# Loading the 64-row remainders of Wq and Wk by 16 heads with their halves swapped, and V rows on GpSimd's queue, in a fused attention and FFN kernel

## The chip, the cores and the metric

The kernel runs on one core of a Trainium2 chip, in one launch. The metric is the device time of that launch in microseconds (us), the median of several runs; lower is better.

The core's engines have names that recur below. PE (TensorE) multiplies matrices, and PEld is its loading of weights. DVE (VectorE), ACT (ScalarE) and POOL (GpSimd) work on elements. SP (SyncE) only issues DMA transfers; ACT and POOL can issue them too. The memory next to the engines has 128 partitions; a transfer or a matmul uses all of them, or a part.

## The reference

Four blocks run in turn on x (2048 rows of 576, bf16): attention, FFN, the same attention and the same FFN again with the same weights. Each takes a layer norm of x and adds its result to x.

```python
def _A_ref(x, mem0, Wq, Wk, Wv, Wo, seg_len):        # 32 heads of 128, seg_len 32, 8 rows of memory
    ...
    mem = mem0
    for s in range(n_seg):                            # 64 segments
        xs = x[:, s * seg_len:(s + 1) * seg_len, :].copy()
        h = jnp.concatenate([mem, xs], axis=1)        # 40 rows
        q = jnp.einsum('btd,dhe->bhte', h, Wq)
        k = jnp.einsum('btd,dhe->bhte', h, Wk)
        v = jnp.einsum('btd,dhe->bhte', h, Wv)
        scores = jnp.einsum('bhqe,bhke->bhqk', q, k) * scale
        scores = jnp.where(mask[None, None], scores, -1000000000.0)
        p = _softmax(scores, axis=-1)
        o = jnp.einsum('bhqk,bhke->bhqe', p, v)
        o = jnp.einsum('bhte,hed->btd', o, Wo)
        mem = o[:, :M, :].copy()
        outs.append(o[:, M:, :])
    return jnp.concatenate(outs, axis=1)

def _B_ref(x, w1, w3, w2):                            # 576 -> 4608 -> 576
    h = _silu(x @ w1) * (x @ w3)                      # shortened
    return h @ w2

x = x + _A_ref(_layernorm(x), A_mem0, ...)
x = x + _B_ref(_layernorm(x), ...)
x = x + _A_ref(_layernorm(x), A_mem0, ...)
x = x + _B_ref(_layernorm(x), ...)
```

The memory rows make the attention a recurrence: a segment needs the output of the one before it.

## The kernel before

**Steps.** One step is one segment of 32 rows. The second attention runs 8 segments behind the first, so that there are 72 steps; in steps 8 to 63 both layers have a segment and their rows stand side by side as the moving side of one matmul (80 columns: twice 8 + 32). The FFN of both layers runs in pieces of 128 rows between the attention's parts.

**One step of attention.** The 32 heads go in four groups of 8 (`g` = 0 to 3). For each group the kernel makes Q and K (`QK` and its remainder `QKt`), the scores, a softmax on DVE and ACT, a transpose of P, PV, and with Wo the output. Where both layers run, P goes into a buffer PB that POOL has filled with zeros (`pb_zero`, a memset of 128x1024 of 0.95 us), DVE multiplies the softmax into it, and SP transposes it by DMA into PTS (`ptr_dma`). PV multiplies PTS with V. There are two buffers each of PB and PTS.

**Rows of 576.** The contraction over 576 rows goes as four full chunks of 128 and a remainder of 64. Wq and Wk lie in the tile W, `[128, 9, 4096]`: chunks 0 to 3 are Wq's full chunks, 4 to 7 Wk's, and chunk 8 holds the remainders: Wq's in partitions 0 to 63, Wk's in 64 to 127, each 4096 columns (32 heads of 128). `qk_tail` (node `QKt`) multiplies them. For each head it issues one matmul on the lower half of PE's rows (Wq) and one on the upper half (Wk); such row-tiled matmuls on different halves can run side by side. The FFN has row-tiled remainders of its own (`FFt`). A group of them in PE's order thus goes lower, upper, lower, upper.

**What sets the order.** `make_nodes` writes the work as nodes with costs and dependencies. PE's order is a fixed string of letters, one for each node. `plan` simulates the engines with the costs and fixes in which order ACT, DVE, POOL and SP issue their nodes; the costs in the nodes move only this order. The program then runs with semaphores.

**Loads.** SP loads the weights at the start in the order of the node's priorities: Wv, the first rows of x (XN), `load_qt` (both remainders of Wq and Wk, two transfers of 64x4096), Wq's and Wk's full chunks for heads 0 to 15 (8 transfers of 128x2048), those for heads 16 to 31, and Wo. The FFN's weights (tiles W13 and W2C; `W<-in_B_w_dram` in the profile, W_83 for W13 in the order's rows) don't stay: SP loads them again and again, on the same queue as the transposes. POOL issues the loads of x for the residual (XR), some stores, and a step of the layer norm (L950).

**V rows.** For the first layer's segments 9 to 16 V is computed ahead and stored in DRAM (XV). `va_load` (node `VAl`, 4 for each of 8 steps, 32 in all, 32x1024 or 64 KB each) loads the rows back into V by SP's queue. A load for step t + 1 and group g waits for PV of step t and group g, which reads the rows that it overwrites.

Of the kernel before, what the change touches and what calls it, by code (L numbers as in the profile page):

```python
# [9 lines left out]
ACT = mybir.ActivationFunctionType  # L10
# [3 lines left out]
P = 128  # L14
R64 = 64
D = 576
NCH = D // R64
H = 32
E = 128
MEM = 8  # L20
SEG = 32
# [5 lines left out]
GROUPS = ((0, 8), (8, 8), (16, 8), (24, 8))  # L27
# [5 lines left out]
R_HT = 6  # L33
PTR = 112
VAT = -9.5
LOAD_BW = {"ldqk": 400e3, "ldv": 410e3, "ldo": 360e3}
AH = (8, 17)
AROWS = (AH[0] + 1) * SEG
TRLAT = 2.5
# [29 lines left out]
def role(t):  # L69

    return (t - LAG) % 2
# [199 lines left out]
def make_nodes(em, nseg, pools, o=Opt, dma_bw=230e3, load_bw=380e3, tail_bw=330e3):  # L271
# [24 lines left out]
    def load(name, nbytes, prio, fn, deps=()):  # L296
        return node("DMA", nbytes / LOAD_BW.get(name, load_bw), fn, deps=deps, prio=prio, name=name, lat=2.0)

    ld_m0 = node("ACT", 0.1, em.load_m0(), prio=-90, name="m0", lat=8.0)
    ld_t = [node("DMA", 1.3, em.load_vt(0), prio=-10.0, name="ldt", lat=2.0), node("ACT", 0.1, em.load_vt(1), prio=-80, name="ldt", lat=9.0)]  # L300
    ld_qt = node("DMA", 3.0, em.load_qt(), prio=-9.2, name="ldt", lat=2.0)
    ld_qk = [load("ldqk", kb(1024, H // 2 * E), i - 9.0, em.load_qk(i)) for i in (0, 1)]
    ld_h = [ld_qk[h0 // (H // 2)] for h0, _ in GROUPS]
    ld_v = [load("ldv", kb(512, 2048), VAT + 0.1 * i, em.load_v(i)) for i in (0, 1)]
# [3 lines left out]
    stored = []  # L308
    b = banks(1)
# [42 lines left out]
    vx_ev, last_v, pvs = {}, [], {}  # L352
# [46 lines left out]
    def step(t):  # L399
# [19 lines left out]
        for g, (h0, nh) in enumerate(GROUPS):  # L419
            qs, qe = [], []  # L420
            for uh, un in units(g, nl):
                q = Slot("qkt", users=1)
                b = banks()
                pq = t + o.qk + o.ustep * uh / 4
                m_ = node("PE", 8 * un * mmq, em.qk(t, uh, un, b), deps=hx + hm[:1] + ([ld_h[g]] if t == 0 else []),
                          prio=pq, mode="full", acq=[q] + b, name="QK")
                n = node("PE", un * mmq, em.qk_tail(t, uh, un, b), deps=hx + hm + ([ld_h[g], ld_qt] if t == 0 else []), prio=pq + o.qkt, mode="row",
                         acq=[q] + b, name="QKt")
# [13 lines left out]
            a = node("DVE", dve(w40), em.sm_add(t, g, s, sme), deps=[sc], prio=pf, rel=[s], name="add")  # L442
            m_ = node("DVE", dve(w40, w40) + 0.13, em.sm_max(t, g, sme), deps=[a], prio=pf, name="maxsub")
            c = node("ACT", 0.105 + w40 * 0.000833, em.sm_exp(t, g, sme), deps=[m_], prio=pf, name="exp")
            pb = Slot("pb")
            d = node("DVE", dve(w40) + 0.23, em.sm_sum(t, g, sme), deps=[c], prio=pf, name="sum")
            w = (1.04 - 0.07 * (e and not pre(t)) if nl == 2 else 0.46) * nh / 8
            pbs = node("DVE", w, em.sm_pb(t, g, sme, pb), deps=[d], prio=pf, acq=[pb], rel=[sme], name="pb")
            pts = Slot("pts")
            if nl == 2:  # L450
                tr = node("DMA", 1.25 * nh / 8, em.ptr_dma(t, g, pb, pts), deps=[pbs], prio=pf - 0.02, acq=[pts], name="TR", lat=TRLAT, ring=TRX)
            else:
                bt = banks(1)
# [12 lines left out]
            ot = [Slot("ot") for _ in range(nl)]  # L466
            if pre(t) and t > AH[0]:
                kept = [d for blk in blks for d in vx_ev["VM", t - 1, blk]]
                if t < AH[1]:
                    kept.append(node("DMA", 0.3, em.va_load(t, g), deps=stored + [pvs[t - 1, g]], prio=t - 1 + o.gstep * g + 0.2, lat=2.4, ring=0.6, name="VAl"))  # L470
            else:
                kept = [d for blk in blks for d in vx_ev["VX", t - e, blk]]
            pv = node("PE", nh * mm80, em.pv(t, g, pts, b), deps=pe_ + kept + [d for blk in blks for d in vx_ev["VM", t, blk]],
                      prio=pf + o.pv, mode="full/col", acq=b + ot, rel=[pts], name="PV")
            pvs[t, g] = pv
            if paired(t):
                for blk in blks:
                    gb, gd = vgs[blk // 2]
                    vx_ev["VX", t + 1, blk] = vg_out(t, blk, gb, gd + [pv], 0)
            ote = [node("AD", ew(w40), em.ot_ev(t, g, ab, b[ab], ot[ab]), deps=[pv], prio=pf, rel=[b[ab]], name="OTe") for ab in range(nl)]  # L480
            wo = node("PE", 4 * nh * mm80, em.wo(t, g, ot), deps=ote + ([ld_o[g]] if t == 0 else []), prio=t + o.wo + o.wog * h0 / 8, mode="full",
                      acq=[y] if g == 0 else [], name="WO")
# [32 lines left out]
    kept = {}  # L515
# [195 lines left out]
class Emitter:  # L711
# [98 lines left out]
        return lambda n: (self.adma if r else self.dma)(self.wv(True)[r * R64:(r + 1) * R64, :].rearrange("p (q n) -> p q n", q=NV),  # L810
                                                        self.a.wv[4 * P:D, :].rearrange("p (q r n) -> r p q n", q=NV, r=2)[r])

    def load_qt(self):
        def f(n):
            for r, wd in ((0, self.a.wq), (1, self.a.wk)):
                self.dma(self.T.W[r * R64:(r + 1) * R64, 8, :], wd[4 * P:D, :])
        return f

    def wv(self, tail):
# [304 lines left out]
    def va_load(self, t, g):  # L1124

        def f(n):
            r0, row = (t - AH[0] - 1) * SEG, 96 * role(t)
            self.dma(self.T.V[row:row + SEG, 2 * g:2 * g + 2, :], self.T.XV[r0:r0 + SEG, g * 1024:(g + 1) * 1024].rearrange("p (b n) -> p b n", n=512))
        return f

    def at(self, t):
# [32 lines left out]
    def qk_tail(self, t, uh, un, b):  # L1164
        def f(n):
            first = self.begin(b)
            for j in range(un):
                e0 = (uh + j) * E
                for kind in (0, 1):
                    rr = slice(kind * R64, (kind + 1) * R64)  # L1170
                    x, w = self.qk_rhs(t, rr, 4)
                    self.mm(self.bk(b[kind])[:, j * w:(j + 1) * w], self.T.W[rr, 8, e0:e0 + E], x,
                            first and j == 0, True, tile_position=(kind * R64, 0))
        return f

    def qk_ev(self, t, un, r, q, b):
# [459 lines left out]
```

## Time and profile before

| | |
|---|---|
| median of 3 runs | 2638.43 us (2637.35 to 2639.35) |
| profiled execution | 2643.07 us |
| its span, first to last instruction | 2641.3 us |
| around the span | 1.8 us |
| mean granted TensorE clock | 0.994 |
| busy: PE / DVE / ACT / POOL | 97% / 77% / 46% / 13% |
| mean DMA rate | 142 GB/s |

The span is cut into views: busy shares of the engines, the chain of work that ended last (followed back from the last instruction to what released each step), groups of instructions, waits, and timelines. L735 is the line through which all matmuls are issued, L741 that of DVE, L738 of ACT, L744 SP's DMAs, L753 POOL's DMAs, L1280 the memset of PB, L1290 the transpose by DMA. In a timeline's row stand the start, the duration, the engine, line and operation, output<-input, the count of like instructions, and in brackets the idle time before and what ended it.

### The profile page before, as it was taken

The numbers are of one execution on the slowest core, as the hardware profiler recorded it, in microseconds if no ns is written. First come the engines' busy times: TensorE is split into PE (matmuls) and PEld (weight loads), VectorE is DVE, ScalarE is ACT, GpSimd is POOL, SyncE is SP. The second block draws the span as 40 slices with busy tenths as digits, with TensorE's granted clock in tenths as the row PEclk, the third lists the DMA queues.
The fourth block names the chain that finished last, engine by engine and source line by source line (L and its number), as shares of the span: only waits on it lengthen the run. The fifth ranks groups of instructions, "written<-read, shape, count | busy, mean of one in ns | idle before, by whom it ended". The sixth has DMA issues, their size and how long they took to land.

```text
span 2641.3 us, 132672 instructions
## 1 busy us (share of the span) xinstructions
PE 2563.1 (97%) x58964; PEld 2182.5 (83%) x58991; DVE 2042.3 (77%) x5156; ACT 1225.3 (46%) x3492; POOL 338.1 (13%) x401
## 2 busy tenths in 40 slices
PE   6999999999999999999999999999999999999998
PEld 4788778888888888888888888888888888888887
DVE  5778777787888778778877877887787777788866
ACT  2545444544445354444535444453544445454543
POOL 1111111110111111111101101111111111011110
PEclk8999999999999999999999999999999999999999
DMA  9155747556555667555464655655575555554457
GB/s 308 56 154 139 183 106 179 143 134 155 129 135 115 151 127 155 134 132 138 110 144 126 158 137 126 146 112 139 120 166 134 135 135 112 135 121 141 127 156 239
DMA packets 690960, 375.94 MB, mean 142 GB/s; under 512 B 234728, under 2 KB 683248, under 8 KB 690128
## 3 DMA queue, kind: packets, MB, share of 16 engines
q1 hardware_dynamic: 686784, 359.94, 55.6%
q8 instruction: 461, 7.55, 1.2%
q0 software_dynamic: 3024, 6.93, 1.0%
q14 instruction: 115, 0.94, 0.1%
q10 hardware_dynamic: 576, 0.57, 0.1%
HBM read 309.11 MB, written 4.46 MB: 119 GB/s over the span
## 4 chain that ended last, share of the span: by engine, by line
PE 86%; DMA 7%; DVE 5%; issue 1%; ACT 1%; SPq 0%; POOL 0%; ACTq 0%; DVEq 0%; POOLq 0%
PE bank L735 86%; DMA PTS<-PB 2%; DMA W<-in_B_w_dram 1%; DMA W<-in_A_Wk_dram 1%; DVE STAT L741 1%; DMA W2C<-in_B_w_dram 1%; DVE SME L741 1%; DVE PB L741 1%; DVE V L741 1%; DVE HTT L741 1%; DMA WV<-in_A_Wv_dram 0%; ACT V L738 0%; SPq L744 0%; DVE QKT L741 0%; DVE XR L741 0%
## 5 line engine op out<-in xcount | busy, mean ns | idle before, releaser
L735 PEld LDWEIGHTS <-W 128*128 128x128 bf16 (+2 forms) x31776 | 1241.3, 100 | 131.8 <-issue 68.6
L735 PE MATMUL bank<-HT,W 128*128 128x80 bf16 (+2 forms) x23040 | 792.0, 197 | 16.6 <-issue 6.1
L735 PE MATMUL bank<-XTB,W 128*64 128x256 bf16 (+5 forms) x8736 | 661.4, 263 | 5.9 <-DMA W<-in_B_w_dram 3.1
L1280 POOL MEMSET PB<- 128x1024 bf16 x288 | 273.7, 951 | 1728.1 <-DMA PTS<-PB 950.9
L738 ACT ACTIVATE QKT<-bank 128x192 bf16<-128x192 f32 (+2 forms) x1505 | 356.0, 319 | 294.9 <-PE bank L735 286.0
L735 PE MATMUL bank<-OT,WO 128*128 128x80 bf16 (+3 forms) x11520 | 419.0, 198 | 5.7 <-issue 3.6
L735 PEld LDWEIGHTS <-WO 128*128 128x128 bf16 (+1 forms) x11520 | 386.4, 102 | 42.0 <-issue 30.0
L738 ACT ACTIVATE V<-bank 32x512 bf16<-32x512 f32 (+1 forms) x545 | 311.7, 586 | 164.7 <-PE bank L735 151.5
L735 PE MATMUL bank<-WV,HT 128*32 128x512 bf16 (+5 forms) x3777 | 347.7, 383 | 3.2 <-issue 2.5
L738 ACT ACTIVATE HTT<-bank 128x512 bf16<-128x512 f32 (+1 forms) x326 | 177.3, 549 | 312.6 <-PE bank L735 311.2
L735 PE MATMUL bank<-W2C,HTT 128*64 128x288 bf16 (+1 forms) x3224 | 314.8, 287 | 6.3 <-DMA W2C<-in_B_w_dram 2.9
L741 DVE TENSOR_REDUCE STAT<-SME 104x8 f32<-104x320 f32 (+1 forms) x576 | 274.7, 477 | 26.7 <-ACT SME L738 18.3
L741 DVE SCALAR_TENSOR_TENSOR XR<-bank,XR 128x288 f32<-128x288 f32 x574 | 242.1, 448 | 62.3 <-PE bank L735 57.6
L741 DVE TENSOR_TENSOR PB<-SME,STAT 40x128 bf16<-40x128 f32 (+4 forms) x932 | 276.6, 332 | 11.6 <-DVE STAT L741 0.4
L735 PEld LDWEIGHTS <-HTT 128*64 128x64 bf16 (+1 forms) x3304 | 226.5, 106 | 45.6 <-issue 8.7
L741 DVE SCALAR_TENSOR_TENSOR HTT<-HTT,bank 128x512 bf16<-128x512 bf16 (+1 forms) x324 | 200.8, 620 | 62.8 <-ACT HTT L738 59.7
L735 PEld LDWEIGHTS <-HT 128*32 128x32 bf16 (+5 forms) x3800 | 138.5, 101 | 128.5 <-issue 21.7
L738 ACT ACTIVATE OT<-bank 128x320 bf16<-128x320 f32 (+2 forms) x409 | 157.4, 399 | 172.6 <-PE bank L735 165.9
L741 DVE CAST V<-bank 64x512 bf16<-64x512 f32 (+1 forms) x287 | 196.6, 685 | 41.4 <-PE bank L735 35.4
L741 DVE TENSOR_TENSOR HTT<-HTT,bank 128x512 bf16<-128x512 bf16 (+1 forms) x324 | 203.6, 628 | 29.3 <-PE bank L735 0.9
L738 ACT ACTIVATE SME<-SME 104x320 f32<-104x320 f32 (+1 forms) x288 | 135.3, 470 | 173.3 <-DVE SME L741 171.7
L741 DVE CAST QKT<-bank 128x192 bf16<-128x192 f32 (+4 forms) x415 | 122.1, 335 | 89.7 <-PE bank L735 86.5
(64 smaller groups left out, 1413.5 us busy)
## 6 DMA issues: line engine op xcount, KB each, us to landing
W<-in_B_w_dram SPq DMA_DIRECT2D x608, 256.0 KB, 3.8
W2C<-in_B_w_dram SPq DMA_DIRECT2D x304, 288.0 KB, 3.9
W<-in_B_w_dram SPq DMA_DIRECT2D x608, 32.0 KB, 3.5
W<-in_B_w_dram SPq DMA_DIRECT2D x16, 512.0 KB, 6.9
W<-in_A_Wq_dram SPq DMA_DIRECT2D x9, 512.0 KB, 10.2
W<-in_A_Wk_dram SPq DMA_DIRECT2D x9, 512.0 KB, 10.2
WO<-in_A_Wo_dram SPq DMA_DIRECT2D x4, 1152.0 KB, 14.3
XR<-in_A_x_dram POOLq DMA_DIRECT2D x16, 288.0 KB, 3.1
```

Source lines behind the costliest of these rows:

```text
L735: self.ch("PE", self.nc.tensor.matmul(out, lhsT=lhsT, rhs=rhs, start=start, stop=stop, skip_group_check=True, **k))
L738: self.ch("ACT", self.nc.scalar.activation(*a, **k))
L741: self.ch("DVE", getattr(self.nc.vector, fn_)(*a, **k))
L1280: return lambda n: self.ch("POOL", self.nc.gpsimd.memset(self.T.PB[:, pb.i, 0:GROUPS[g][1]], 0.0))
```

## The change

Three things change; the letters of PE's order don't.

1. `load_qt(i)` loads the remainders by 16 heads, i = 0 and 1, in two transfers of 64x2048 each. In chunk 8 columns 0 to 2047 now hold Wq's and columns 2048 to 4095 Wk's. For heads 0 to 15 Wq lies in the lower half of the partitions and Wk in the upper, as before; for heads 16 to 31 it is the other way round. Each piece stands in SP's order ahead of the full chunks of its heads, and QKt in step 0 waits for its own piece. `qk_tail` still issues Wq's matmul first, so for heads 16 to 31 a group now goes upper, lower, upper, lower.
2. `va_load` issues on POOL (`swdma`, engine SWD in the plan) instead of SP.
3. Some costs in the plan are other numbers.

```diff
-LOAD_BW = {"ldqk": 400e3, "ldv": 410e3, "ldo": 360e3}
+LOAD_BW = {"ldqk": 405e3, "ldv": 405e3, "ldo": 357e3}
...
-    ld_t = [node("DMA", 1.3, em.load_vt(0), prio=-10.0, name="ldt", lat=2.0), ...
-    ld_qt = node("DMA", 3.0, em.load_qt(), prio=-9.2, name="ldt", lat=2.0)
+    ld_t = [node("DMA", 3.0, em.load_vt(0), prio=-10.0, name="ldt", lat=2.0), ...
+    ld_qt = [node("DMA", 2.6, em.load_qt(i), prio=i - 9.2, name="ldt", lat=2.0) for i in (0, 1)]
     ld_qk = [load("ldqk", kb(1024, H // 2 * E), i - 9.0, em.load_qk(i)) for i in (0, 1)]
...
-                n = node("PE", un * mmq, em.qk_tail(t, uh, un, b), deps=hx + hm + ([ld_h[g], ld_qt] if t == 0 else []), ...
+                n = node("PE", un * mmq, em.qk_tail(t, uh, un, b), deps=hx + hm + ([ld_h[g], ld_qt[GROUPS[g][0] // (H // 2)]] if t == 0 else []), ...
...
-                    kept.append(node("DMA", 0.3, em.va_load(t, g), deps=stored + [pvs[t - 1, g]], prio=..., lat=2.4, ring=0.6, name="VAl"))
+                    kept.append(node("SWD", 1.0, em.va_load(t, g), deps=stored + [pvs[t - 1, g]], prio=..., lat=4.0, name="VAl"))
...
-    def load_qt(self):
-        def f(n):
-            for r, wd in ((0, self.a.wq), (1, self.a.wk)):
-                self.dma(self.T.W[r * R64:(r + 1) * R64, 8, :], wd[4 * P:D, :])
+    def load_qt(self, i):
+        def f(n):
+            w = H // 2 * E
+            for kind, wd in ((0, self.a.wq), (1, self.a.wk)):
+                r0 = (kind ^ i) * R64
+                self.dma(self.T.W[r0:r0 + R64, 8, kind * w:(kind + 1) * w], wd[4 * P:D, i * w:(i + 1) * w])
...
-            self.dma(self.T.V[row:row + SEG, 2 * g:2 * g + 2, :], self.T.XV[...])
+            self.swdma(self.T.V[row:row + SEG, 2 * g:2 * g + 2, :], self.T.XV[...])
...
     def qk_tail(self, t, uh, un, b):
         def f(n):
             first = self.begin(b)
             for j in range(un):
-                e0 = (uh + j) * E
+                up, hh = divmod(uh + j, H // 2)
                 for kind in (0, 1):
-                    rr = slice(kind * R64, (kind + 1) * R64)
+                    r0 = (kind ^ up) * R64
+                    rr, e0 = slice(r0, r0 + R64), (kind * H // 2 + hh) * E
                     x, w = self.qk_rhs(t, rr, 4)
                     self.mm(self.bk(b[kind])[:, j * w:(j + 1) * w], self.T.W[rr, 8, e0:e0 + E], x,
-                            first and j == 0, True, tile_position=(kind * R64, 0))
+                            first and j == 0, True, tile_position=(r0, 0))
```

**On SP at the start of the program**, the difference of the orders (W is the tile of Wq and Wk, XN the first rows of x):

```order
 L744 DMA XN<-in_A_x_dram 128x576
-L744 DMA W<-in_A_Wq_dram 64x4096
-L744 DMA W<-in_A_Wk_dram 64x4096
+L744 DMA W<-in_A_Wq_dram 64x2048
+L744 DMA W<-in_A_Wk_dram 64x2048
 L744 DMA W<-in_A_Wq_dram 128x2048 x4
 L744 DMA W<-in_A_Wk_dram 128x2048 x4
+L744 DMA W<-in_A_Wq_dram 64x2048
+L744 DMA W<-in_A_Wk_dram 64x2048
 L744 DMA W<-in_A_Wq_dram 128x2048 x4
 L744 DMA W<-in_A_Wk_dram 128x2048 x4
```

Half of the remainders' bytes have moved from ahead of all full chunks to between the first eight and the second eight.

**On POOL in steps 8 and 9**, before: the memsets of PB, four a step, with a load of XR between them.

```order
L950 TENSOR_TENSOR LNS<-LNS,mhalf 128x1 x2
L1280 MEMSET PB 128x1024 x5
L753 DMA XR<-in_A_x_dram 128x576
L1280 MEMSET PB 128x1024
L950 TENSOR_TENSOR LNS<-LNS,mhalf 128x1
L1280 MEMSET PB 128x1024 x6
```

The same place after the change (its line numbers are 2 or 3 higher):

```order
L952 TENSOR_TENSOR LNS<-LNS,mhalf 128x1 x2
L1283 MEMSET PB 128x1024 x2
L753 DMA V<-XV 32x1024 x2
L1283 MEMSET PB 128x1024
L753 DMA V<-XV 32x1024
L1283 MEMSET PB 128x1024
L753 DMA V<-XV 32x1024
L1283 MEMSET PB 128x1024
L753 DMA XR<-in_A_x_dram 128x576
L1283 MEMSET PB 128x1024
L753 DMA V<-XV 32x1024 x2
```

The V loads stand between the memsets of PB; from here to step 16 there is one for nearly each memset.

**On SP at that place**, before, with transposes of P, the FFN's weights and V loads in one queue:

```order
L1290 DMA_TRANSPOSE PTS<-PB 128x8x112
L744 DMA W_83<-in_B_w_dram 64x256 x2
L744 DMA V<-XV 32x1024 x2
L744 DMA W_83<-in_B_w_dram 64x256 x2
L1290 DMA_TRANSPOSE PTS<-PB 128x8x112
L744 DMA W_83<-in_B_w_dram 128x4x256 x2
L744 DMA V<-XV 32x1024
```

and after:

```order
L1293 DMA_TRANSPOSE PTS<-PB 128x8x112
L744 DMA W_83<-in_B_w_dram 64x256 x4
L1293 DMA_TRANSPOSE PTS<-PB 128x8x112
L744 DMA W_83<-in_B_w_dram 128x4x256 x4
```

The V loads are gone, and the FFN's weight loads close up. PE's rows are the same in both programs, but for the halves that the remainders of heads 16 to 31 use.

More of the change, by code (lines that the diff above doesn't have):

```diff
@@ L299, in make_nodes @@
     ld_m0 = node("ACT", 0.1, em.load_m0(), prio=-90, name="m0", lat=8.0)
-    ld_t = [node("DMA", 1.3, em.load_vt(0), prio=-10.0, name="ldt", lat=2.0), node("ACT", 0.1, em.load_vt(1), prio=-80, name="ldt", lat=9.0)]
-    ld_qt = node("DMA", 3.0, em.load_qt(), prio=-9.2, name="ldt", lat=2.0)
+    ld_t = [node("DMA", 3.0, em.load_vt(0), prio=-10.0, name="ldt", lat=2.0), node("ACT", 0.1, em.load_vt(1), prio=-80, name="ldt", lat=9.0)]
+    ld_qt = [node("DMA", 2.6, em.load_qt(i), prio=i - 9.2, name="ldt", lat=2.0) for i in (0, 1)]
     ld_qk = [load("ldqk", kb(1024, H // 2 * E), i - 9.0, em.load_qk(i)) for i in (0, 1)]
@@ L426, in step @@
                           prio=pq, mode="full", acq=[q] + b, name="QK")
-                n = node("PE", un * mmq, em.qk_tail(t, uh, un, b), deps=hx + hm + ([ld_h[g], ld_qt] if t == 0 else []), prio=pq + o.qkt, mode="row",
+                n = node("PE", un * mmq, em.qk_tail(t, uh, un, b), deps=hx + hm + ([ld_h[g], ld_qt[GROUPS[g][0] // (H // 2)]] if t == 0 else []), prio=pq + o.qkt, mode="row",
                          acq=[q] + b, name="QKt")
@@ L469, in step @@
                 if t < AH[1]:
-                    kept.append(node("DMA", 0.3, em.va_load(t, g), deps=stored + [pvs[t - 1, g]], prio=t - 1 + o.gstep * g + 0.2, lat=2.4, ring=0.6, name="VAl"))
+                    kept.append(node("SWD", 1.0, em.va_load(t, g), deps=stored + [pvs[t - 1, g]], prio=t - 1 + o.gstep * g + 0.2, lat=4.0, name="VAl"))
             else:
@@ L1127, in f @@
             r0, row = (t - AH[0] - 1) * SEG, 96 * role(t)
-            self.dma(self.T.V[row:row + SEG, 2 * g:2 * g + 2, :], self.T.XV[r0:r0 + SEG, g * 1024:(g + 1) * 1024].rearrange("p (b n) -> p b n", n=512))
+            self.swdma(self.T.V[row:row + SEG, 2 * g:2 * g + 2, :], self.T.XV[r0:r0 + SEG, g * 1024:(g + 1) * 1024].rearrange("p (b n) -> p b n", n=512))
         return f
```

## The prediction

> **What bounds the kernel now.** I read the page first: the engines' shares, then the shares of the chain that ended last.
>
> ```profile
> PE 2563.1 (97%) x58964; PEld 2182.5 (83%) x58991; DVE 2042.3 (77%) x5156; ACT 1225.3 (46%) x3492; POOL 338.1 (13%) x401
> PE 86%; DMA 7%; DVE 5%; issue 1%; ACT 1%; SPq 0%; POOL 0%; ACTq 0%; DVEq 0%; POOLq 0%
> ```
>
> TensorE is busy 97% of the span and carries 86% of the chain. PE's order is a fixed string that the change leaves alone, so the time can move in three ways only: PE waits less or more for weights at the start, it waits less or more for something that SP or POOL issue in steps 9 to 16, or the same matmuls run closer or wider because the halves of the array come in another order. I take these as three terms. All of this is one profiled execution of 2643.07 us, 4.64 above the median of 2638.43; the sum is made on the former and the 4.64 is taken off at its end. A difference under 0.2% (5.3 us) counts as no change.
>
> **Term 1, the start.** The chain of waits of the first 110 us, and PE's timeline there (start, duration, in brackets the idle time before and who ended it):
>
> ```profile
> 14.28 13.22 DMA W<-in_A_Wk_dram
> 27.51 9.93 DMA W<-in_A_Wk_dram
> 37.46 10.20 DMA W<-in_A_Wk_dram
> 47.70 1.94 PE bank L735 x73
> ...
> 37.49 2.17 PE L735 MATMUL bank<-HT,W 128*128 128x40 bf16 x73 [1.09 <-DMA W<-in_A_Wk_dram]
> 47.70 1.89 PE L735 MATMUL bank<-HT,W 128*128 128x40 bf16 x73 [0.57 <-DMA W<-in_A_Wk_dram]
> ```
>
> The chain runs on DMA until 47.70: PE starts the first 16 heads' QK when the first half of Wq and Wk has landed (37.49, after 1.09 idle) and those of heads 16 to 31 when the second has (47.70, after 0.57 idle). Before both, in the old order, stand the two remainders of 64 partitions x 4096. What they cost is in the windows (after the window: its length, busy time of PE, PEld, DVE, ACT, POOL, then granted clock, DMA share, GB/s):
>
> ```profile
> 14.00:18.00 4.00, 4.00 (x22) 1.74 (x20) 0.00 (x0) 0.00 (x0) 0.00 (x0) 1.00 1.13 402
> 18.00:21.00 3.00, 2.33 (x31) 1.14 (x27) 0.00 (x0) 1.32 (x6) 0.00 (x0) 1.00 0.94 142
> 21.00:24.00 3.00, 0.00 (x0) 0.00 (x0) 1.74 (x8) 1.11 (x3) 0.55 (x1) 1.00 1.02 218
> 24.00:27.00 3.00, 2.67 (x22) 1.34 (x24) 1.45 (x4) 0.00 (x0) 0.00 (x0) 0.62 1.00 279
> 32.00:37.00 5.00, 3.30 (x59) 1.26 (x50) 3.99 (x6) 4.03 (x7) 0.00 (x0) 1.00 1.03 409
> ```
>
> From 18 to 27 us the engines of the DMA are full (0.94 to 1.02) and move only 3 x (142 + 218 + 279) = 1917 KB; at the 409 GB/s of the 128-partition loads that takes 4.7 us. So the two remainders (1.05 MB) cost 9 - 4.7 = 4.3 us more than their bytes. The change puts half of them behind the first half's main loads. For the first half that saves 0.52 MB / 409 = 1.3 plus half the surcharge, 2.15: its weights land some 3.4 us earlier. But PE then only waits longer at the next gate: it still needs the second half, and ahead of that stands the same number of bytes. The second gate moves only by what the surcharge shrinks when the later two pieces run mixed with main loads of all 128 partitions. Bounds: nothing (0), or the whole of that half (-2.15). No row shows a 64-partition load between 128-partition ones, so I take the middle, **-1.0**. The chain is DMA up to 47.70, so what is saved there is saved at the end.
>
> The Trainium skill speaks against more (SBUF — State Buffer, "Can I just issue two DMAs to hit both halves?"): two transfers, one on each half of the partitions, run one after the other, only 6% better than one. By that page the second gate stays where it is, term 1 is 0 and the sum below comes out 1.0 higher. Our 142 to 218 GB/s, with a lower and an upper piece queued one behind the other, agrees with it.
>
> **Term 2, the V rows.** 32 loads leave SP's queue and go to POOL's. What SP spends on them, and what PE waits for between 255 and 560 us (in total, times, longest):
>
> ```profile
> L744 SPq DMA_DIRECT2D V<-XV x32: 303/452/1367, 269.0 to 526.1; - x32
> PE bank L735 <- DMA PTS<-PB: 5.4, 4, 2.2
> PE bank L735 <- DMA W<-in_B_w_dram: 0.6, 2, 0.3
> PE bank L735 <- DMA W2C<-in_B_w_dram: 0.2, 1, 0.2
> ```
>
> SP gets 32 x 0.45 = 14 us back, but SP is no bound; what counts is whether a P transpose (PTS) or a weight load waited behind a V load. All DMA waits here are 5.4 + 0.6 + 0.2 = 6.2 us, so the gain ends at -6.2. The four PTS waits one by one, the two longest with the queue before them:
>
> ```profile
> 275.81 0.45 PE L735 MATMUL bank<-PTS,V 128*128 128x80 bf16 x8 [1.74 <-DMA PTS<-PB]
> 349.56 0.74 PE L735 MATMUL bank<-PTS,V 128*64 128x80 bf16 x16 [2.19 <-DMA PTS<-PB]
> 377.29 0.45 PE L735 MATMUL bank<-PTS,V 128*128 128x80 bf16 x8 [1.15 <-DMA PTS<-PB]
> ...
> 270.11 1.64 SPq L744 DMA_DIRECT2D W<-in_B_w_dram  x2
> 271.85 1.25 SPq L1290 DMA_TRANSPOSE PTS<-PB  x1
> ...
> 341.49 3.18 SPq L744 DMA_DIRECT2D W<-in_B_w_dram  x4
> 344.77 1.24 SPq L1290 DMA_TRANSPOSE PTS<-PB  x1
> ```
>
> The transposes behind the two longest were issued at 271.85 and 344.77, right behind FFN weight loads, which the change leaves on SP; the third (377.29) was issued once a PV had freed its buffer. None stands right behind a V load. I take **-0.3**, a tenth of the first two's 3.9 rounded down, for V loads further up the queue.
>
> On the other side, V(t+1, g) now stands on POOL between two memsets of the P buffer, and waits there for PV(t, g). Queued behind it: the memset of the next group, behind that DVE's mask multiply into PB, the transpose and the next PV. Step 11 is the tightest that I found:
>
> ```profile
> 372.05 0.97 PE L735 MATMUL bank<-PTS,V 128*64 128x80 bf16 x32
> 372.64 0.95 POOL L1280 MEMSET PB<- 128x1024 bf16 x1 [4.40 <-DMA PTS<-PB]
> 374.80 1.13 DVE L741 TENSOR_TENSOR PB<-SME,STAT 40x256 bf16<-40x256 f32 x4
> 300.14 0.57 POOL L753 DMA_DIRECT2D XR<-in_A_x_dram  x1
> ```
>
> This memset ended at 373.59 and DVE needed it at 374.80: 1.2 us to spare. Of the 32 matmuls at 372.05 the first 16 are the older group; PV(11, 0) ends at about 372.5. A V load behind it, at the 0.57 us that POOL's own XR load takes to issue, ends at about 373.1, and the memset at 374.1: still 0.7 to spare. So the cost is 0 if a V load holds POOL for no more than about 1.3 us (0.57 + 0.7); the upper bound, one such step late by a little in each of eight, is about +1. I add nothing.
>
> **Term 3, the halves of the array.** For heads 16 to 31 each pair of remainder matmuls now comes as upper, lower instead of lower, upper. In PE's order there are 227 places (from the letters) where such a group stands next to another row-tiled group, so that two matmuls of the same half now follow each other: lower, upper, upper, lower. What that costs depends on whether the two of a pair truly start together:
>
> ```profile
> 1005.53 0.31 PE L735 MATMUL bank<-HT,W 64*128 64x80 bf16 x8
> 1005.67 0.38 PE L735 MATMUL bank<-XTB,W 64*128 64x256 bf16 x4
> 1005.89 0.20 PE L735 MATMUL bank<-HT,W 64*128 64x80 bf16 x2
> ...
> 1009.77 1.91 PE L735 MATMUL bank<-XTB,W 128*128 128x256 bf16 x16
> 1011.52 0.65 PE L735 MATMUL bank<-W2C,HTT 128*128 128x288 bf16 x4
> ```
>
> Eight of 80 columns take 1005.67 - 1005.53 = 0.14, so 35 ns a pair; four of 256 take 0.22, so 110 ns a pair. A full-array matmul of 256 columns comes every (1011.52 - 1009.77) / 16 = 109 ns, and one lasts 1.91 - 15 x 0.109 = 0.27. The group of four lasts 0.38 = 0.109 + 0.27 + the offset within a pair: that offset is 0.00, at the 10 ns to which the rows are given. If the two halves start together, it does not matter which is named first: at a clash the second upper one waits for the end of the first, and its lower partner starts with it. So a clash costs 0 to 10 ns; I take 3, 227 x 0.003 = **+0.7** (ends 0 and +2.3).
>
> **The sum.** 2643.07 - 1.0 - 0.3 + 0.7 = 2642.5; minus 4.64 gives **2637.8**. DVE's and ACT's orders differ only in the first steps, SP's FFN remainders move up by the places that V loads leave, and the last SP loads keep their order: those I cost at nothing, with PE's own queue as cover.
>
> **The rivals.**
>
> *Slower: every clash costs a slot.* If weights for a half can't be loaded while that half still computes, the second of two equal halves waits out a whole pair slot of 35 ns: 227 x 0.035 = +8.0, so 2638.43 - 1.0 - 0.3 + 8.0 = **2645.1**. For it: no row of the trace shows two equal halves in a row, so the offset of 0.00 speaks of the old order alone. Against it: in the old order each third matmul of a run already follows one of its own half at full pace. It decides against no change (over +5.3) from (5.3 + 1.3) / 227 = 29 ns a clash. The Trainium skill (TensorE: Matmul & The Clock Gate, "Step-by-step: what each phase is for") lets a weight load be pulled ahead when row groups don't conflict or when it goes to the background weights; by the first alone this rival would hold, by the second the forecast does. The full-array rows above, whose weights do load behind a running matmul, bear out the second.
>
> *Slower: POOL holds the memsets.* If a V load holds POOL for 2.5 us instead of 0.57, each memset in steps 9 to 16 behind one is late by 2.5 - 1.3 = 1.2 where the slack is that of step 11; one such delay reaching PE in each of eight steps is +9.6, less 1.3: **2646.7**. The page of the profile speaks against it: XR loads by POOL land after 3.1 us, as soon as those by SP:
>
> ```profile
> XR<-in_A_x_dram POOLq DMA_DIRECT2D x16, 288.0 KB, 3.1
> ```
>
> The Trainium skill (SBUF — State Buffer, "Who interferes with whom") speaks for it: GpSimd writes the descriptors of its own DMAs and is locked out while DVE runs in a two-port mode. With DVE at 77% that could stretch an issue; the 0.57 here shows none of it.
>
> *Faster: the remainders run at full rate, and SP's stalls go.* If both pieces of the second half hide behind main loads (-2.15), and the two transposes behind SP's weight loads are on time (1.74 + 2.19 = 3.9), with no clash cost: 2638.43 - 2.15 - 3.9 = **2632.4**.
>
> *No gain at the start* (the second gate stays): **2638.8**. Here also lies the granted clock, which is 0.50 in two windows:
>
> ```profile
> 59.00:64.00 5.00, 4.31 (x108) 3.55 (x105) 1.61 (x5) 1.36 (x3) 1.62 (x2) 0.50 0.22 61
> 64.00:68.00 4.00, 3.60 (x126) 3.50 (x123) 0.99 (x4) 1.11 (x4) 0.00 (x0) 0.50 0.89 338
> ```
>
> PE's wait ahead of the second half grows from 0.57 to about 0.57 + 3.4 - 1.0 = 3.0 us; should the clock fall after it as it did here, the 4 to 5 us that follow cost about 2 more, 2640. Equally those 9 us could shift by chance: 4 us either way. Both stay about within 0.2%.
>
> **How the numbers follow.** Forecast 0.48; no gain at the start 0.13; faster rival 0.15; clashes 0.13; POOL 0.11. A twentieth of the forecast's cases falls past either bound (0.02 each): faster 0.17, same 0.57, slower 0.26. The range goes from the faster rival, 2632.4, to just past the clash rival, 2645.5; beyond lie about half of the faster rival and two thirds of the POOL one, some 0.15.
>
> **What would show it.** Right: the second half's first QK group at about 46.7 with 2 to 3 us of idle before it, the first half's at about 34; PTS waits between 255 and 560 near 5 us; POOL's V loads near 0.57 each; in a steady step such as 1005 the row-tiled groups with 35 ns a pair. Wrong: PE's idle time "issue" or its busy time up by some 8 us spread evenly over all steps (clashes); POOL's memsets ending after DVE wanted them in steps 9 to 16; half clock over more of the first 70 us.

## The result, and the profile after

| | before | after |
|---|---|---|
| median of 18 runs each | 2638.50 us (2634.36 to 2644.71) | 2642.49 us (2636.41 to 2651.75) |
| ratio after / before | | 1.0018, 95% interval 1.0010 to 1.0026 |
| profiled execution | 2643.07 us | 2641.68 us |

The change is slower by 0.18%: by the ratio 4.7 us, between 2.6 and 6.9. That is inside the 0.2% that the prediction counted as no change and inside its range, but it is clear of zero, and the forecast was 0.6 faster. The two profiled executions stand the other way round (before's was 4.6 over its median, after's 0.8 under its own), so their totals explain nothing; what counts is what each shows at a place. First the page of after, its span, shares and chain:

```profile
span 2639.9 us, 132720 instructions
PE 2564.1 (97%) x58991; PEld 2182.7 (83%) x58991; DVE 2044.2 (77%) x5155; ACT 1225.9 (46%) x3493; POOL 353.5 (13%) x433
PE 84%; DMA 7%; DVE 6%; issue 1%; ACT 1%; SPq 0%; POOL 0%; ACTq 0%; DVEq 0%; POOLq 0%
```

PE bounds the kernel as before. **The start**, PE's timeline and the windows (length, busy times, granted clock, DMA share, GB/s) of after:

```profile
35.31 2.42 PE L735 MATMUL bank<-HT,W 128*128 128x40 bf16 x73 [2.14 <-DMA W<-in_A_Wk_dram]
47.51 1.96 PE L735 MATMUL bank<-HT,W 128*128 128x40 bf16 x73 [1.05 <-DMA W<-in_A_Wk_dram]
...
18.00:24.00 6.00, 3.48 (x47) 1.86 (x45) 2.81 (x10) 2.82 (x8) 0.55 (x1) 1.00 1.02 275
24.00:28.00 4.00, 4.00 (x38) 1.54 (x38) 0.69 (x1) 0.91 (x2) 0.00 (x0) 1.00 1.03 409
28.00:34.00 6.00, 4.25 (x79) 1.77 (x71) 3.80 (x6) 3.91 (x7) 0.00 (x0) 1.00 1.04 311
34.00:38.00 4.00, 2.69 (x75) 2.28 (x75) 1.90 (x4) 1.03 (x3) 0.00 (x0) 0.68 1.02 294
```

There are now two dips of the rate: one at the first pair of pieces (275 GB/s) and a second, between 28 and 38 us, at the second pair (311 and 294), where before moved 409. The DMA engines are full in all of them (1.02 to 1.04). The first half's QK starts at 35.31 instead of 37.49, the second half's at 47.51 instead of 47.70.

**The V loads**: POOL's loads, its timeline in step 11, and what PE waits for between 255 and 560 us:

```profile
L753 POOL DMA_DIRECT2D V<-XV x32: 496/496/549, 263.4 to 521.2; - x32
...
366.44 0.50 POOL L753 DMA_DIRECT2D V<-XV  x1
370.17 0.95 POOL L1283 MEMSET PB<- 128x1024 bf16 x1 [3.23 <-DMA PTS<-PB]
371.31 0.50 POOL L753 DMA_DIRECT2D V<-XV  x1 [0.20 <-DVE OT L741]
371.80 0.97 POOL L1283 MEMSET PB<- 128x1024 bf16 x1
...
PE bank L735 <- DMA PTS<-PB: 3.4, 4, 2.0
PE bank L735 <- DVE HTT L741: 1.8, 3, 1.2
PE bank L735 <- DMA W<-in_B_w_dram: 0.2, 1, 0.2
```

A V load holds POOL for 0.50 us by the median of the 32 and 0.55 at most, so the lock-out that the Trainium skill describes (SBUF — State Buffer, "Who interferes with whom") does not show, and P transposes are waited for 3.4 us instead of 5.4.

**The halves of the array**: row-tiled matmuls with their count and busy time, of before:

```profile
L735 PE MATMUL bank<-HT,W 64*128 64x80 bf16 x3584 | 113.4, 199 | 0.7 <-DVE HT L741 0.6
L735 PE MATMUL bank<-XTB,W 64*128 64x256 bf16 x1008 | 88.2, 271 | 1.2 <-DMA W<-in_B_w_dram 0.7 <-DVE XR L741 0.5
```

and of after:

```profile
L735 PE MATMUL bank<-HT,W 64*128 64x80 bf16 x3584 | 113.5, 199 | 0.7 <-DVE HT L741 0.6
L735 PE MATMUL bank<-XTB,W 64*128 64x256 bf16 x1008 | 88.8, 271 | 0.8 <-DVE HTT L741 0.4 <-DMA W<-in_B_w_dram 0.2
```

0.1 and 0.6 us more over the whole program: the clashes cost next to nothing. (A sum of 0.7 is no measure of them, though: before's own second profile, e12 below, has 113.7 and 88.7, which is 0.8 more without any swap.)

**The end** holds what the prediction did not see. PE's and SP's timelines of after, from 2569 us:

```profile
2579.72 2.70 PE L735 MATMUL bank<-HT,W 64*128 64x40 bf16 x80 [3.58 <-DMA W<-in_B_w_dram]
...
2569.82 0.90 SPq L744 DMA_DIRECT2D W2C<-in_B_w_dram  x2
2572.02 6.54 SPq L744 DMA_DIRECT2D W<-in_B_w_dram  x5
2582.45 0.37 SPq L744 DMA_DIRECT2D WV<-in_B_w_dram  x1
```

and the same matmuls in before, with nothing in brackets:

```profile
2579.07 2.07 PE L735 MATMUL bank<-HT,W 64*128 64x40 bf16 x80
```

These are QKt of the last step. At the end of the program SP loads the last FFN's weights over Wq and Wk in tile W, in pieces of 512 columns, each as soon as the group of heads that owned these columns in the old layout is done (`tail_load`). In the new layout columns 0 to 511 of chunk 8 hold Wq's remainder of heads 0 to 3 in the lower half and of heads 16 to 19 in the upper, but the load still waits for the first alone. It now stands ahead of QKt of heads 16 to 19 in the program, and QKt waits for it to land: 3.58 us. This is more than a wait. In the last segment of the second attention these four heads multiply with FFN weights in place of the 64 rows of Wq's remainder, so the changed kernel computes something else there than the kernel before. e2 below shares that, and in e5 it is the remainders of both Wq and Wk. The wait is in the program's order too: the row of PE that loads the first weights of these matmuls reads, in after,

```order
L735 LDWEIGHTS W [waits DMAHW1_49]
```

and in before it has no such wait on a DMA. PE's rows thus differ in more than the halves that the remainders use.

### The profile page after: what moved, and what is told of

Read it like the earlier page. It is cut to its first block, busy times and chain, and to the rows that moved or that the text cites. A ratio compares the mean times of both kernels' runs of the same rounds, so it can differ in the third digit from the quotient of the medians.

```text
span 2639.9 us, 132720 instructions
## 1 busy us (share of the span) xinstructions
PE 2564.1 (97%) x58991; PEld 2182.7 (83%) x58991; DVE 2044.2 (77%) x5155; ACT 1225.9 (46%) x3493; POOL 353.5 (13%) x433
## 4 chain that ended last, share of the span: by engine, by line
PE 84%; DMA 7%; DVE 6%; issue 1%; ACT 1%; SPq 0%; POOL 0%; ACTq 0%; DVEq 0%; POOLq 0%
PE bank L735 84%; DMA PTS<-PB 3%; DMA W<-in_B_w_dram 2%; DVE STAT L741 1%; DVE SME L741 1%; DVE PB L741 1%; DMA W<-in_A_Wk_dram 1%; DMA W2C<-in_B_w_dram 1%; DVE HTT L741 1%; DVE V L741 1%; DMA W<-in_A_Wq_dram 0%; DMA WV<-in_A_Wv_dram 0%; ACT V L738 0%; DVE QKT L741 0%; DVE XR L741 0%
## 5 line engine op out<-in xcount | busy, mean ns | idle before, releaser
L741 DVE TENSOR_REDUCE STAT<-SME 104x8 f32<-104x320 f32 (+1 forms) x576 | 274.5, 476 | 25.5 <-ACT SME L738 17.1
```

Of the source, the lines that this page charges most:

```text
L741: self.ch("DVE", getattr(self.nc.vector, fn_)(*a, **k))
```

## The experiments

Letters for the parts: S the split of the remainders' loads, W the swap of halves, P the plan costs, V the V loads on POOL, T the shared columns at the end, F four pieces of 64x2048 ahead of all full chunks. Each was timed against before on the same chip. The last two columns are from each kernel's profile: when the second half's first QK group started, and QKt's wait at the end.

| kernel | parts | median, us | before, us | ratio (95%) | second half, us | wait at end, us |
|---|---|---|---|---|---|---|
| after | S W P V T | 2642.49 | 2638.50 | 1.0018 (1.0010 to 1.0026) | 47.51 | 3.58 |
| e1 | S W P V | 2644.00 | 2639.67 | 1.0017 (1.0005 to 1.0028) | 47.92 | none |
| e2 | W T F | 2641.28 | 2639.67 | 1.0013 (1.0002 to 1.0024) | 44.93 | 3.17 |
| e3 | V | 2638.43 | 2639.67 | 1.0006 (0.9994 to 1.0018) | 46.38 | none |
| e4 | S W P | 2642.60 | 2639.67 | 1.0016 (1.0006 to 1.0025) | 48.13 | none |
| e5 | T F | 2641.67 | 2639.24 | 1.0006 (0.9996 to 1.0016) | 46.28 | 3.91 |
| e6 | W F | 2638.45 | 2639.24 | 0.9997 (0.9984 to 1.0010) | 45.96 | none |
| e7 | S P | 2641.65 | 2639.24 | 1.0010 (0.9998 to 1.0021) | 47.01 | none |
| e8 | P | 2640.30 | 2639.24 | 1.0001 (0.9988 to 1.0013) | 45.37 | none |
| e9 | W V F | 2638.93 | 2639.87 | 0.9996 (0.9984 to 1.0007) | 45.74 | none |
| e10 | S W P V | 2644.46 | 2639.87 | 1.0016 (1.0004 to 1.0029) | 49.14 | none |
| e11 | on ACT's queue | 2638.99 | 2639.87 | 1.0004 (0.9992 to 1.0015) | 47.33, no wait | none |
| e12 | before again | 2642.62 | 2639.87 | one run | 47.56 | none |
| f1 | S | 2635.89 | 2634.16 | 1.0004 (0.9992 to 1.0016) | 47.72 | none |
| f2 | F | 2637.54 | 2634.16 | 1.0010 (1.0002 to 1.0019) | 46.08 | none |
| f3 | F P V | 2634.99 | 2634.16 | 0.9998 (0.9989 to 1.0008) | 46.85 | none |

**e1**, the changed kernel with each head's remainders in its own columns (no T):

```diff
-                self.dma(self.T.W[r0:r0 + R64, 8, kind * w:(kind + 1) * w], wd[4 * P:D, i * w:(i + 1) * w])
+                self.dma(self.T.W[r0:r0 + R64, 8, i * w:(i + 1) * w], wd[4 * P:D, i * w:(i + 1) * w])
...
-                    rr, e0 = slice(r0, r0 + R64), (kind * H // 2 + hh) * E
+                    rr, e0 = slice(r0, r0 + R64), (up * H // 2 + hh) * E
```

> The changed kernel with one index changed: in chunk 8 both remainders of a head lie in the head's own columns (Wq and Wk of heads 0 to 15 in columns 0 to 2047, those of heads 16 to 31 in 2048 to 4095), halves still swapped for heads 16 to 31, loads and V rows as in the changed kernel. Theory A (the loss is a wait near the end: FFN weights loaded into chunk 8 now share columns with heads 16 to 31, and QKt of the last step waits for such a load, 3.58 us in the changed kernel's trace): that wait is gone and the time is 3 to 4 us under the changed kernel, 2638 to 2639. Theory B (the V loads on POOL cost it) and theory C (the clashes of equal halves cost it): no wait there either, but the time stays some 4 us above before, about 2642.5.

The wait at the end went. PE's timeline there:

```profile
2577.83 2.00 PE L735 MATMUL bank<-HT,W 64*128 64x40 bf16 x76
```

but the kernel stayed at 1.0017. Theory A as the whole cause falls.

**e2**, before with the new layout and its four pieces in front:

```diff
-            for r, wd in ((0, self.a.wq), (1, self.a.wk)):
-                self.dma(self.T.W[r * R64:(r + 1) * R64, 8, :], wd[4 * P:D, :])
+            for i in (0, 1):
+                for kind, wd in ((0, self.a.wq), (1, self.a.wk)):
+                    r0 = (kind ^ i) * R64
+                    self.dma(self.T.W[r0:r0 + R64, 8, kind * w:(kind + 1) * w], wd[4 * P:D, i * w:(i + 1) * w])
```

> The kernel before with the new layout of chunk 8 alone: remainders in four pieces of 64x2048 but all ahead of the full chunks, V rows on SP, plan costs as before. Theory A: a wait of about 3 to 4 us for an FFN weight load at QKt of the last step, and 3 to 4 us more than before, about 2642. Theory B: as before, 2638.5. Theory C: 4 us more than before, but without the wait.

The wait is there (3.17) and the kernel is slower than before, as theory A has it for this part, though by 1.6 us between the medians and not by 3 to 4.

**e3**, before with V loads on POOL:

```diff
-            self.dma(self.T.V[row:row + SEG, ...
+            self.swdma(self.T.V[row:row + SEG, ...
```

> The kernel before with the V loads on POOL alone. Theory A and theory C: 0 to -1 us against before (2637.5 to 2638.5), P transposes waited for between 255 and 560 us some 2 to 5 us. Theory B: about 4 us more than before, and memsets of PB that end after DVE wanted them.

No loss that can be told from none, but the interval reaches 1.0018, so this run alone does not rule out the 4 us of theory B; e4, still slow without the V loads on POOL, and e9 and f3, as fast as before with them, do. P transposes were waited for 5.6 us, no less than before.

**e4**, e1 with the V loads back on SP (e3's diff, reversed):

> The kernel of e1 with the V loads back on SP: what is left of the change is the split of the remainders' loads, the swap of halves and the plan costs. Theory A: 0 to -1 us against before; second half of the weights at PE at 47.5, as in the changed kernel (47.51), so the start gives 0.2 at most. Theory B: the same. Theory C: some 4 us more than before.

Slower by as much as e1, with the second half at 48.13 and not at 47.5. V is not the cause; S, W or P is.

**e5**, before with heads 16 to 31 in columns 0 to 2047 of chunk 8 and heads 0 to 15 behind them, halves as before:

```diff
+                    r0 = kind * R64
+                    self.dma(self.T.W[r0:r0 + R64, 8, (1 - i) * w:(2 - i) * w], wd[4 * P:D, i * w:(i + 1) * w])
...
+                    rr, e0 = slice(r0, r0 + R64), ((1 - up) * H // 2 + hh) * E
```

> The kernel before with one thing changed: in chunk 8 the remainders of heads 16 to 31 lie in columns 0 to 2047 and those of heads 0 to 15 in 2048 to 4095, halves as before (no swap), four pieces ahead of the full chunks, V rows on SP. The FFN weights loaded at the end into columns 0 to 511 then meet heads 16 to 19, as in the changed kernel. Theory A (wait near the end): QKt of the last step waits 3 to 4 us for such a load, and the time is 2.5 to 4 us above before. Theory C (swap of the halves) and theory D (the split load order at the start or the plan costs): as before.

Without any swap the wait at the end comes back, at the same matmuls:

```profile
2580.16 2.60 PE L735 MATMUL bank<-HT,W 64*128 64x40 bf16 x80 [3.91 <-DMA W<-in_B_w_dram]
```

That the shared columns make it is shown. The median is 2.4 us up, the ratio 1.0006 with no change inside its interval.

**e6**, e2 in the heads' own columns: the swap without T.

> The kernel before with the halves swapped for heads 16 to 31 and nothing else: own columns, so no wait near the end; four pieces ahead of the full chunks, V rows on SP. Theory A: 0 to +1 us against before. Theory C: +3 to +4 us against before. Theory D: as before.

0.9997, with an interval up to 1.0010 (2.6 us): theory C falls by the time too.

**e7**, e4 without the swap (`r0 = kind * R64` at both places).

> The kernel of e4 without the swap: remainders loaded by 16 heads next to the full chunks, halves as before, plan costs as in the changed kernel, V rows on SP. Theory A: 0 to -1 us against before. Theory C: the same. Theory D: +3 to +4 us against before, already there when step 8 begins.

The loss of theory D is there without the swap, but smaller: 1.0010, with no change just inside the interval.

**e8**, before with after's plan costs.

> The kernel before with the changed plan costs alone (rates of the loads 405, 405 and 357, the Wv remainder's node 3.0, the Wq and Wk remainders' node 5.2): only a few of DVE's and ACT's instructions in the first steps change places. Theories A and C: as before. Theory D in the form that the plan costs are to blame: +3 to +4 us; in the form that the loads' order is: as before.

The plan costs alone do nothing (1.0001), so of theory D the loads' order is left.

**e9**, e6 with the V loads on POOL: the change without split and shared columns.

> The changed kernel without the two suspects: the remainders' four pieces stand ahead of all full chunks again (no split) and lie in the heads' own columns (no wait near the end); the swap of halves and the V loads on POOL stay, plan costs as before. Theory F (the loss is the wait near the end, some 3 us, plus a second half of Wq and Wk that lands some 2 us later because of the split): no QKt wait at the end, the second half's first QK at 45 to 46.4 us, and 0 to -1 us against before. Rival G (something else of the change, spread over the steps, costs the 4 us): still +3 to +4 us.

0.9996: with S and T out, the loss is gone, as theory F has it. The windows of e9 show one dip instead of two, and the second half is early:

```profile
18.00:24.00 6.00, 3.29 (x47) 1.74 (x45) 2.82 (x11) 2.43 (x7) 0.55 (x1) 1.00 1.02 217
24.00:28.00 4.00, 3.95 (x35) 1.56 (x36) 1.06 (x2) 0.60 (x1) 0.00 (x0) 1.00 1.02 396
28.00:34.00 6.00, 4.36 (x78) 1.80 (x70) 3.74 (x6) 3.78 (x7) 0.00 (x0) 1.00 1.02 408
34.00:38.00 4.00, 2.72 (x76) 2.43 (x76) 1.75 (x3) 0.96 (x3) 0.00 (x0) 0.67 1.03 411
...
45.74 1.90 PE L735 MATMUL bank<-HT,W 128*128 128x40 bf16 x73 [0.42 <-DMA W<-in_A_Wk_dram]
```

**e10**, after with the loads at the end waiting for both groups of heads:

```diff
-  ... (4, 0.6, qk_done[i]), ...
+  ... (4, 0.6, qk_done[i] + qk_done[(i + 4) % 8]), ...
```

> The changed kernel with the two 64x512 FFN loads of each of the first three pieces held back, at the end, until both groups of heads that share their columns have done QKt. PE then never waits there, but the loads behind on SP come later. Theory F: QKt's wait of 3.6 us goes; what comes back through later FFN weights is under 1 us, so 2 to 3.5 us under the changed kernel, about +2 against before, with the second half at 47 to 48. Rival G: stays at +4.

The wait is gone, the time is not lower than after's (1.0016 against 1.0018), and the second half came latest of all, at 49.14. The 2 to 3.5 us that it should have won do not show.

**e11**, before with both remainders issued by ACT at the start (`adma`, prio -70).

> The kernel before with the two full remainders (64x4096) issued on ACT's queue at the very start, beside the loads of Wv, and nothing else by intent (DVE's and ACT's first instructions shift a little). Theory F: if 64-partition loads cost more than their bytes only while they stand alone in the queue, mixing hides it and the second half lands 1 to 3 us earlier than 45 to 46.4, and the time is 1 to 3 us under before; if they slow whatever runs beside them, as the split suggests, the second half stays at 45 to 46.4 and the time too. Rival G: as before.

As before within the interval (1.0004). PE started the second half's QK at 47.33 here, in one group of 80 without a wait for a load, so the row does not say when the weights landed, and whether mixing hid anything stays open.

**e12**, before unchanged, one run with a profile.

> The kernel before, unchanged, for a second profile of its start. In its first profile the second half's first QK began at 47.70. Theory F: that was a late one, and this one shows 45 to 46.4, as the other kernels without the split do. Rival G: 47.7 again, and the split then moved nothing.

Theory F's expectation failed here, and what rival G expected came: before again shows its late second half,

```profile
18.00:24.00 6.00, 1.69 (x27) 0.81 (x21) 1.59 (x7) 2.43 (x7) 0.55 (x1) 0.95 0.99 184
...
47.56 1.90 PE L735 MATMUL bank<-HT,W 128*128 128x40 bf16 x73 [0.70 <-DMA W<-in_A_Wk_dram]
```

with one dip that is deeper (184 GB/s here, 217 in e9). So the split's later second half is seen against the other kernels, not against before's own two profiles.

**f1**, before with the split alone; **f2**, before with four pieces in front in the old layout; **f3**, f2 with after's plan costs and V on POOL, the candidate that might beat both.

```diff
 f1:
+            for r, wd in ((0, self.a.wq), (1, self.a.wk)):
+                self.dma(self.T.W[r * R64:(r + 1) * R64, 8, i * w:(i + 1) * w], wd[4 * P:D, i * w:(i + 1) * w])
 f2, f3:
+            for i in (0, 1):
+                for r, wd in ((0, self.a.wq), (1, self.a.wk)):
+                    self.dma(... the same ...)
```

> The kernel before with the split of the remainders' loads alone: same layout, no swap, plan costs as before (1.5 for each half), V rows on SP. SP's order differs from before in the first 20 loads only. Theory F (the split itself delays the second half): the second half's first QK at 47 to 49, the windows between 28 and 38 us at some 300 to 340 GB/s instead of 410, and +2 to +4 us. Rival H (the four other kernels with the split lose by the changed plan costs or by chance): as before.

> The kernel before with the remainders as four pieces of 64x2048, lower and upper in turn, all ahead of the full chunks; nothing else changed. Theory F in the form that pieces matter by their place alone: second half at 45.5 to 47.6 and the time as before (within 1 us). In the form that four pieces in front are better than two: second half at 45 to 46.3 and 1 to 2 us under before. Rival H: as before.

> What the runs so far leave of the change without its losses: four pieces in front in the old layout (no split, no wait near the end), the changed plan costs, V loads on POOL. Theory F: second half at 45 to 46.3, P transposes as in the changed kernel, 1 to 3 us under before and 4 to 7 under the changed kernel. Rival H: as before.

f1 has both dips and the late second half that after has:

```profile
18.00:24.00 6.00, 4.16 (x57) 2.18 (x53) 3.19 (x11) 2.43 (x7) 0.55 (x1) 1.00 1.00 287
28.00:34.00 6.00, 3.29 (x59) 1.34 (x51) 4.87 (x8) 4.70 (x8) 0.00 (x0) 1.00 1.05 307
...
47.72 2.25 PE L735 MATMUL bank<-HT,W 128*128 128x40 bf16 x73 [1.06 <-DMA W<-in_A_Wk_dram]
```

so the second dip comes with the split alone, without swap or plan costs. (A second half as late as 47.72 the kernel before has too, at 47.70.) Its time is 1.0004, as rival H expected and below the +2 to +4 us of theory F, though the interval reaches 1.0016. f2 is slower than before (1.0010, clear of no change) in spite of its earlier second half, which neither form of theory F expected; e6, e9 and f3, with the same four pieces in front, are not. f3 ties with before (0.9998) and misses its 1 to 3 us; nothing beat before.

**Taken together.** The 14 ratios with an interval (e11 left out) fitted by least squares as sums of the six parts, weighted by their intervals, in us of 2640 and with one standard error: S +2.7 ± 1.2, T +1.6 ± 0.9, W +0.6 ± 0.9, P +0.4 ± 1.0, F +0.4 ± 0.7, V -0.3 ± 0.8. The fit takes the parts to add, which no run shows, and the kernels on one chip share one set of before's runs. For the changed kernel it adds up to 5.0, against 4.7 measured. In the profiles, the second half's QK starts at 47.0 to 49.1 (mean 47.9) in the six kernels with S and at 44.9 to 47.7 (mean 46.3, before's two included) in the ten without (e11 left out): 1.6 us later. Against the four of these that load in before's own order (before, e12, e3, e8; mean 46.75) it is 1.15 us, and the ranges overlap. The lateness is carried on: the ninth memset of PB starts at 100.9 us on average in the six and at 99.2 in the ten.

## Why the prediction was wrong, point by point

**Term 1, the start: -1.0 forecast; +1.2 to +1.6 in the profiles, +2.7 ± 1.2 by the fit.** This is the step that failed first: the surcharge of the later two pieces was taken to shrink by half when they run between full loads. It did not shrink. The bounds, 0 to -2.15, excluded a loss, for the reason that the bytes ahead of the second half stay the same. The bytes do, the rate does not: the first dip becomes shallower (275 GB/s in after, 217 in e9 for 18 to 24 us), but a second one opens (from 408 and 411 in e9 to 311 and 294). Lost against 409 between 18 and 38 us: after 6 x 134 + 6 x 98 + 4 x 115 = 1852 KB, e9 6 x 192 + 4 x 13 + 6 x 1 = 1210 KB; the difference of 642 KB is 1.6 us at 409, as much as the second half is late. Summed in the same way, the six kernels with S lose 1616 to 1958 KB and eight without it (e11 left out) 1026 to 1390, but before's own two profiles, with one deep dip, 1782 and 1712. So that there was no gain is sure; that there was a loss rests on the other kernels and on the times. The middle of the bounds was taken in the wrong direction: 64-partition loads between full ones did not hide among them, the rate fell while they ran. The Trainium skill's rule that the prediction set beside this term (SBUF — State Buffer, "Can I just issue two DMAs to hit both halves?") was nearer: next to no gain from using the two halves in turn; that there is a loss it does not say. The first half, forecast 3.4 us earlier, came 0.3 earlier (mean 35.6 with S, 35.9 without). PE did wait longer at the second gate, as the prediction said, but less than its 3.0 us: 1.05 before the main group and 0.97 before the single matmul ahead of it, 2.0 in all, against 0.57.

**Term 2, the V rows: -0.3 forecast; -0.3 ± 0.8 by the fit.** P transposes waited for went from 5.4 to 3.4 us in after but stood at 5.6 in e3; over all profiles the mean is 4.0 in the six with V on POOL (3.2 to 5.6) and 5.2 in the eleven without (2.6 to 6.9), so a gain of this size lies within the scatter. The price taken for a V load on POOL (0.57) was 0.50, and the memsets were in time. The rival in which POOL holds the memsets is refuted.

**Term 3, the halves: +0.7 forecast; +0.6 ± 0.9 by the fit.** The busy times of the two groups sum to 202.6 us on average in the seven profiles with the swap and 202.1 in the ten without, where before's own two differ by 0.8; that the step from before to after is just 0.7 is luck. The rival of a whole slot (+8.0) is refuted by e6, whose interval ends at 2.6 us, 12 ns a clash. With that the offset of 0.00 within a pair told the right story as far as the runs resolve it.

**What the sum left out.** The prediction says that "the last SP loads keep their order: those I cost at nothing". Their order did stay, and that was the trouble: the order was right for the old columns only. SP's rows were compared, but not which of PE's rows now wait for them. QKt's wait of 3.2 to 3.9 us is shown in all three kernels that share columns and whose loads wait for one group alone, and in none of the others. Of its price, +1.6 ± 0.9 by the fit stands against 3.6 in the trace. From the start of the 281st memset of PB, here in before and in after,

```profile
2558.03 0.95 POOL L1280 MEMSET PB<- 128x1024 bf16 x1 [14.49 <-PE bank L735]
```

```profile
2553.74 0.95 POOL L1283 MEMSET PB<- 128x1024 bf16 x1 [14.36 <-PE bank L735]
```

to the end of the span pass 83.3 and 86.2 us; over all profiles 84.9 to 86.2 in the three with the wait and 80.3 to 84.0 in the fourteen without. That is about 3 us, most of the wait; but in the three 8.1 us of that stretch ran at half clock on average, in the fourteen 4.9, so up to 1.6 of the 3 may be the clock's. And where the split stayed in place, a kernel without the wait was hardly faster: after stands at 1.0018, e1 at 1.0017 and e10 at 1.0016.

**What stays open.** The parts fit the total within their errors, but no single part is pinned down by the times to better than 0.7 us: f1 has the split alone at +1 where e1, e4 and e10 have it, with other parts, at +4. That e10 lost its wait and not its time is part of that. Why before's own first dip (180 and 184 GB/s between 18 and 24 us) is deeper than that of e3 and e8 (214 and 216), which load the same pieces in the same order, was not found.

The granted clock, a rival in the prediction, is not settled either. In all six kernels with S a stretch at half clock begins just behind the start of the second half's QK, between 48 and 52 us; of the eleven without S, e3 alone has one there, and the others show none between 42 and 54. In after, f1, before and e9:

```profile
48.00:52.00 4.00, 3.39 (x117) 3.33 (x113) 1.83 (x4) 0.87 (x2) 1.17 (x2) 0.64 1.08 391
48.00:52.00 4.00, 3.39 (x111) 3.31 (x108) 1.34 (x3) 0.87 (x2) 0.68 (x1) 0.55 1.09 391
48.00:52.00 4.00, 3.31 (x131) 3.18 (x128) 2.43 (x8) 0.88 (x2) 1.17 (x2) 1.00 1.07 381
48.00:52.00 4.00, 3.44 (x122) 3.11 (x122) 2.95 (x8) 1.94 (x6) 1.85 (x2) 1.00 1.08 390
```

(0.64 and 0.55 against 1.00 is the clock, the third number from the end.) Over the timed runs the mean granted clock was 0.0008 to 0.0013 below that of before on the same chip in e1, e4, e7, e10 and f1, which have S, 0.0011 and 0.0007 below in e2 and e5, which have the wait at the end, and at most 0.0006 below in e3, e6, e8, e9, f2 and f3. Of 2640 us 0.001 is 2.6 us, as much as the losses themselves. So the kernels that wait more at the start or the end also run at a lower clock. Whether the clock carries part of the loss was not shown: no run held it fixed. The sign that the prediction named, half clock over more of the first 70 us, does not show between the two profiles: 10.2 us in after, 17.1 in before.

## What to carry to other kernels

When data moves to other columns or partitions, follow every later writer of that place, not only its readers: the loads that reuse a buffer carry the old map in their conditions, and comparing the order of one queue does not show a new wait on another engine. Here a narrow load cost more than its bytes where it stood among full ones, and splitting it put that cost at two places instead of one; look at GB/s where the DMA engines are full before and after. For effects of 0.1%, two profiles tell where time goes but not how much, as runs of one kernel differ here by more than the effect.

## What the runs showed of the hardware that was not expected

Transfers of 64 partitions lowered the rate of the core's DMA from about 410 to 294 to 342 GB/s while full-width loads stood on both sides of them (after, f1), with the DMA engines at 1.00 to 1.05 busy. Two row-tiled matmuls of the same half in a row cost nothing that the rows resolve, and by e6's interval at most 12 ns. A load of 64 KB issued by POOL took 0.50 us of POOL and landed after 3.9 us, against 3.5 by SP, with DVE 77% busy. In all 17 profiles the clock fell to half in stretches of 3.4 us or a multiple of it (but for one cut short by the end of the span), 10 to 34 us in all in one execution.
